# q k^T v in four 64x64 tiles of the TensorE array, k and v loaded and multiplied a batch at a time

## The chip, the cores and the metric

The kernel runs on one core of a Trainium2 chip. The metric is the device time of one execution in microseconds (us). Of three runs the kernel before took 1111.66 us in the median (1111.28 to 1112.53). The profile is of a further, profiled execution.

The engines have short names in the profile: PE is TensorE's matmuls, PEld its weight loads, DVE is VectorE, ACT is ScalarE, POOL is GpSimd, SP is SyncE, which issues nearly all DMAs here. A name with a q behind it (SPq) is an engine's queue.

## The reference

Two blocks, in float32. Attention without a softmax, for each of 8 batches and 8 heads (576 tokens of 64), with a root-mean-square norm; then a gated layer over all 4608 tokens:

```
kv  = einsum('bhsd,bhse->bhde', k, v)            # 64 x 64 a head
out = einsum('bhsd,bhde->bhse', q, kv)
x   = out / sqrt(mean(out*out, -1) + 1e-6) * g_norm     # (B,H,S,D) -> (4608, 512)
y   = (sigmoid(x @ w_gate) * (x @ w_val)) @ w_out       # d_ff = 1536
```

The weights arrive as 64-bit floats and are converted on the chip.

## The kernel before

**Attention goes by pairs of heads**, 32 in all, 4 a batch. `attention(n, at_ps)` (L211) returns the steps of pair n in their order, and each caller decides when a step runs:

- `kv_mm`: k^T v of both heads. The 576 tokens lie as 96 partitions with 6 tokens each, so a head takes six matmuls of 96 rows and 64 columns. Head 0 goes to PSUM partitions 0 to 63, head 1 to 64 to 127: two column tiles of the array (L221).
- `kv_out`: two copies on DVE put the two 64x64 results on the diagonal of a 128x128 tile that was cleared once (L227), and the loads of a later pair's k and v are issued (L79).
- `q_mm`, `q_out`: six transposes of q (L235), and a copy on ACT (L240), after which a later pair's q is loaded (L88).
- `u_mm`: q times k^T v of both heads at once, with the block-diagonal tile as the moving operand: five matmuls of 115 or 116 tokens (L250).
- `u_square`, `u_sum`, `u_root`, `u_norm`: the norm, on ACT, DVE, ACT, DVE (L254, L258, L262, L265 to L267).
- `x_mm`, `x_out`: five transposes back (L276), and copies on ACT into `xT`, the input of the gated layer (L285).

**The gated layer goes by chunks of 512 tokens**, nine of them. Chunk 0 is computed with plain matmuls (`Plain`, L380; `second`, L472) while the weights are still being converted. The order of the work in the first stage, with the attention of batches 0 and 1, is written out by hand as a list of tokens (`order`, L411): U3, for one, is `u_mm` of pair 3. `warm` tokens are matmuls without a use.

Chunks 1 to 8 run two layers of 7 instead of 8 products of half-size blocks. In `first_layer_fast` two blocks go side by side, one and two. Each has seven products of two matmuls, in the order p1, p6, p2, p7, p5, p4, p3. `product` (L529) issues the matmuls, and each product has an addition on DVE or a copy or sigmoid on ACT behind it. p1 and p2 accumulate into bank `pa`, p6, p7 and p4 into `pb`, p5 and p3 into `pc`. POOL makes the sums of weights (L515). `second_layer_fast` has products of six matmuls (L613) and stores its output tiles (`store`, L343).

**Attention of later batches fills slots.** Between the products there are calls of `slot()`, each of which takes one step from the queue `fill`. `feed(b)` puts the attention of batch b there, two pairs at a time; chunk c carries batch c+1, so chunks 1 to 6 carry batches 2 to 7, and 7 and 8 carry none. In chunk 1 the sums of the second layer's weights (L672, on DVE) are mixed in.

**PSUM has eight banks.** One tile of two banks (`at`, L353) serves all steps of attention, one after the other, so a step's result has to be read before the next step may write. Six single banks (`mm`, L370) serve the products.

**SBUF:** k and v of later pairs lie in two tiles each of the pool `sb`, q in one. Hidden activations come from the pool `hp`, 21 tiles of 128x512 under the tag gv, in turn; one chunk takes 21.

Of the kernel before, what the change touches and what calls it, by code (L numbers as in the profile page):

```python
# [2 lines left out]

# [16 lines left out]
def kernel(  # L20
# [21 lines left out]


    NU = 5
    M = S // NU
    MU = S - M * (NU - 1)
    UC = 192
    UX = M * 3
# [21 lines left out]
    def ahead(n, late):  # L70
        return (n + 4,) if n + 4 < NE else (n + late,) if n + late >= NE else ()

    def load_kv(n):
        if n >= B * NHP:
            return
        b, h0 = n // NHP, 2 * (n % NHP)
        for name, src in (("k", k), ("v", v)):
            t = (first if n < NE else sb).tile([NP, 2, NJ * HD], FP32, tag=name, name=name, bufs=4 if n < NE else 2)
            nc.sync.dma_start(out=t, in_=src[b, h0:h0 + 2].rearrange("h (p j) d -> p h (j d)", j=NJ))  # L79
            pairs[n][name] = t  # L80

    def load_q(n):
        if n >= B * NHP:
            return
        b, h0 = n // NHP, 2 * (n % NHP)
        t = (first if n < NE else sb).tile([NP, NJ, 2, HD], FP32, tag="q", name="q", bufs=4 if n < NE else 1)
        for e in range(2):
            nc.sync.dma_start(out=t[:, :, e, :], in_=q[b, h0 + e].rearrange("(p j) d -> p j d", j=NJ))  # L88
        pairs[n]["q"] = t

# [102 lines left out]
    kvs = [const.tile([P, P], FP32, name=f"kv{i}") for i in range(2)]  # L193
# [6 lines left out]
    for kv in kvs:  # L200
        nc.vector.memset(kv, 0.0)
# [9 lines left out]
    def attention(n, at_ps):  # L211

        b, m = divmod(n, NHP)
        d = {}

        def kv_mm():
            d["kv"] = ps = at_ps("kv")
            for j in range(NJ):
                js = slice(HD * j, HD * j + HD)
                for e in range(2):  # L220
                    nc.tensor.matmul(ps[HD * e:HD * e + HD, 0, 0:HD], pairs[n]["k"][:, e, js], pairs[n]["v"][:, e, js],  # L221
                                     start=(j == 0), stop=(j == NJ - 1))

        def kv_out():
            for e in range(2):
                es = slice(HD * e, HD * e + HD)
                nc.vector.tensor_copy(out=kvs[n % 2][es, es], in_=d["kv"][es, 0, 0:HD])  # L227
            for i in ahead(n, 2):
                load_kv(i)

        def q_mm():
            d["q"] = ps = at_ps("q")
            for j in range(NJ):
                c0 = NP * (j % JH)
                nc.tensor.transpose(ps[:, j // JH, c0:c0 + NP], pairs[n]["q"][:, j].rearrange("p e d -> p (e d)"),  # L235
                                    ident[0:NP, 0:NP])

        def q_out():
            d["qT"] = sb.tile([P, 2, JH * NP], FP32, tag="qT", name="qT")
            nc.scalar.copy(out=d["qT"], in_=d["q"][:, :, 0:JH * NP])  # L240
            for i in ahead(n, 1):
                load_q(i)

        def u_mm():

            ps = at_ps("u")
            d["u"] = ps[0:MU].rearrange("p i c -> p (i c)")[:, 0:NU * UC].rearrange("p (i c) -> p i c", c=UC)[:, :, 0:P]
            qT = d["qT"].rearrange("p i n -> p (i n)")
            for i in range(NU):
                nc.tensor.matmul(d["u"][:, i], qT[:, M * i:M * i + MU], kvs[n % 2], start=True, stop=True)  # L250

        def u_square():
            d["sq"] = sb.tile([MU, NU, P], FP32, tag="sq", name="sq")
            nc.scalar.activation(out=d["sq"], in_=d["u"], func=AF.Square)  # L254

        def u_sum():
            d["ms"] = sb.tile([MU, NU, 2], FP32, tag="ms", name="ms")
            nc.vector.tensor_reduce(out=d["ms"].rearrange("p i e -> p (i e)"),  # L258
                                    in_=d["sq"].rearrange("p i (e d) -> p (i e) d", d=HD), axis=AX.X, op=ALU.add)

        def u_root():
            nc.scalar.activation(out=d["ms"], in_=d["ms"], func=AF.Sqrt, bias=eps[0:MU], scale=1.0 / HD)  # L262

        def u_norm():
            nc.vector.reciprocal(d["ms"], d["ms"])  # L265
            d["xn"] = d["sq"]
            nc.vector.tensor_tensor(out=d["xn"].rearrange("p i (e d) -> p i e d", d=HD),  # L267
                                    in0=d["u"].rearrange("p i (e d) -> p i e d", d=HD),
                                    in1=d["ms"].unsqueeze(3).to_broadcast([MU, NU, 2, HD]), op=ALU.mult)

        def x_mm():
            d["x"] = ps = at_ps("x")
            for i in range(NU):
                m_ = MU if i == NU - 1 else M
                bank, c0 = divmod(M * i, UX)
                nc.tensor.transpose(ps[:, bank, c0:c0 + m_], d["xn"][0:m_, i, :], ident[0:m_, 0:m_])  # L276

        def x_out():

            s0 = 0  # L280
            while s0 < S:
                c, o = divmod(S * b + s0, G)
                i, r = divmod(s0, UX)
                n_ = min(G - o, (UX if i == 0 else S - UX) - r)
                nc.scalar.activation(out=chunk(c)[:, m, o:o + n_], in_=d["x"][:, i, r:r + n_], func=AF.Copy, scale=g_col)  # L285
                s0 += n_

        return [kv_mm, kv_out, q_mm, q_out, u_mm, u_square, u_sum, u_root, u_norm, x_mm, x_out]


# [6 lines left out]
    def feed(b, at_ps):  # L297

        for n in range(NHP * b, NHP * b + NHP, 2):
            both = []  # L300

            def tile_of(i, both=both):
                def ps(kind):
                    if kind != "kv":
                        return at_ps(kind)
                    if not both:
                        both.append(at_ps(kind))
                    return both[0][:, :, HD * i:HD * i + HD]
                return ps

            one, two_ = (attention(n + i, tile_of(i)) for i in range(2))

            def kv_of_both(one=one, two_=two_):
                one[0]()
                two_[0]()

            fill.extend([kv_of_both, one[1], two_[1]])
            for steps in (one, two_):

                fill.extend(steps[2:-2] + [lambda: None] * 2 + steps[-2:])  # L320
# [26 lines left out]

    psum_at = ctx.enter_context(tc.tile_pool(name="psum_at", bufs=1, space=bass.MemoryType.PSUM))
    psum_ctx = tc.tile_pool(name="psum0", bufs=1, space=bass.MemoryType.PSUM)
    psum0 = psum_ctx.__enter__()  # L350

    def at_ps(kind):
        return psum_at.tile([P, 2, 512], FP32, tag="at", name="at")  # L353
# [15 lines left out]
    def mm_ps():  # L369
        return psum.tile([P, 512], FP32, tag="mm", name="mm", bufs=6)  # L370
# [52 lines left out]
    two0 = at_ps(None)  # L423
    for token in order.split():
# [3 lines left out]
        if name == "b":  # L428
            if f not in blks:
# [4 lines left out]
                else:  # L434
                    t = at_ps(None) if f else two0
# [30 lines left out]
    for f in range(4, NFT):  # L466
        plain(0, f, (mm_ps(), mm_ps()))

    ps = [mm_ps() for _ in range(G // P)]
# [48 lines left out]
    def first_layer_fast(c):  # L518
        s, a = sx[c], quarters(c)

        def block(f):

            d = {}
            pa, pb, pc = (mm_ps()[:, h1] for _ in range(3))
# [8 lines left out]
            def p1():  # L533
                product(pa, bg[:, 0:NK], a[1, 1], True)
                d["sg"] = sg_tile()
                nc.scalar.copy(out=d["sg"][:, h2], in_=pa)  # L536

            def p6():
                product(pb, tw[f, 2], s[:, 1], True)
                d["h"] = gv_tile(c, f)  # L540
                tt(out=d["h"][:, h1], in0=pb, in1=d["sg"][:, h2], op=ALU.add)  # L541

            def p2():
                product(pa, bg[:, NK:], a[1, 2], False)
                nc.scalar.activation(out=d["sg"][:, h1], in_=pa, func=AF.Sigmoid)  # L545

            def p7():
                product(pb, tw[f, 3], a[2, 1], False)
                tt(out=d["h"][:, h2], in0=pb, in1=d["sg"][:, h2], op=ALU.add)  # L549

            def p5():
                product(pc, tw[f, 1], s[:, 0], True)
                tt(out=d["h"][:, h2], in0=pc, in1=d["h"][:, h2], op=ALU.add)

            def p4():
                product(pb, tw[f, 4], a[2, 2], False)
                tt(out=d["sg"][:, h2], in0=pb, in1=d["sg"][:, h2], op=ALU.add)  # L557
                nc.scalar.activation(out=d["sg"][:, h2], in_=d["sg"][:, h2], func=AF.Sigmoid)  # L558

            def p3():  # L560
                product(pc, bv[:, NK:], s[:, 2], False)
                tt(out=d["h"][:, h1], in0=pc, in1=d["h"][:, h1], op=ALU.add)  # L562
# [37 lines left out]
    def second_layer_fast(c):  # L600
        b = {(j, n): w2[:, NF2 * (j - 1):NF2 * j, DH * (n - 1):DH * n] for j in (1, 2) for n in (1, 2)}
        d1, d2 = slice(0, DH), slice(DH, DM)
        for g in range(2):
# [5 lines left out]
            pcs = [mm_ps()[:, 0:x.stop - x.start] for x in parts]  # L609
# [20 lines left out]
            for pc, x in zip(pcs, parts):  # L630
# [5 lines left out]
            store(c, 2 + g, o2)  # L636
            for pc, x in zip(pcs, parts):
# [42 lines left out]
    for c in range(1, NG):  # L680
        if c + 1 < B:
            feed(c + 1, at_ps)
        if c == 1:
# [3 lines left out]
            while w2_sums or steps:  # L687
                fill.append(w2_sums.popleft() if w2_sums and len(fill) % 7 in (3, 4) else steps.pop(0))
# [34 lines left out]
```

## Time and profile before

| what | value |
|---|---|
| median of three runs | 1111.66 us |
| the profiled execution: its time, its span | 1112.95 us, 1111.2 us |
| TensorE busy | 99% of the span |
| granted TensorE clock, mean | 0.998 |
| chunk 2 (with a batch's attention), first product to that of chunk 3 | 120.81 us |
| chunk 7 (without) | 108.78 us |
| mean duration of a record of L221, L250 | 224 ns, 273 ns |
| DMA, first two of 40 slices; mean over the span | 248 and 265 GB/s; 52 GB/s |

A line of the profile names the source line, the engine, the operation, the tiles as out<-in, the shape, and how many instructions of that kind it covers (x48). For matmuls, 96*64 means 96 rows and 64 columns of the array. Durations of matmuls are from entry to the end of the result, so neighbours overlap: how long one occupies the array is read from the difference of two starts. Each matmul of float32 shows up as two records, each transpose as one.

### The profile page before, as it was taken

The numbers are of one execution on the slowest core, as the hardware profiler recorded it, in microseconds if no ns is written. First come the engines' busy times: TensorE is split into PE (matmuls) and PEld (weight loads), VectorE is DVE, ScalarE is ACT, GpSimd is POOL, SyncE is SP. The second block draws the span as 40 slices with busy tenths as digits, with TensorE's granted clock in tenths as the row PEclk, the third lists the DMA queues.
The fourth block names the chain that finished last, engine by engine and source line by source line (L and its number), as shares of the span: only waits on it lengthen the run. The fifth ranks groups of instructions, "written<-read, shape, count | busy, mean of one in ns | idle before, by whom it ended". The sixth has DMA issues, their size and how long they took to land.

```text
span 1111.2 us, 15257 instructions
## 1 busy us (share of the span) xinstructions
PE 1101.6 (99%) x5830; PEld 920.2 (83%) x5830; DVE 571.6 (51%) x1159; ACT 318.7 (29%) x615; POOL 280.8 (25%) x390
## 2 busy tenths in 40 slices
PE   8999999999999999999999999999999999999998
PEld 7644458888888888888888888888888888888888
DVE  4887847753365415552455336551556256615541
ACT  4654323321243213330333124321333022101110
POOL 0000024540244204440343024420444044404420
PEclk9999999999999999999999999999999999999999
DMA  9954412021202020201211020203000000010001
GB/s 248 265 175 151 152 40 52 12 54 31 73 12 54 17 75 22 54 12 29 63 40 37 19 73 12 54 12 81 22 11 1 19 19 1 1 29 10 1 1 39
DMA packets 71912, 57.61 MB, mean 52 GB/s; under 512 B 40864, under 2 KB 65824, under 8 KB 71840
## 3 DMA queue, kind: packets, MB, share of 16 engines
q1 hardware_dynamic: 71584, 56.61, 19.2%
q8 instruction: 47, 0.77, 0.3%
q14 instruction: 25, 0.20, 0.1%
q10 hardware_dynamic: 256, 0.03, 0.0%
HBM read 47.19 MB, written 9.44 MB: 51 GB/s over the span
## 4 chain that ended last, share of the span: by engine, by line
PE 96%; DVE 1%; SPq 1%; DMA 1%; ACT 0%; issue 0%; DVEq 0%
PE mm L529 51%; PE mm L613 26%; PE mm L380 6%; PE mm L472 4%; PE at L250 2%; PE at L380 2%; PE at L221 2%; PE at L235 1%; PE at L276 1%; DMA q<-in_q_dram 1%; PE two L250 1%; PE two L221 0%; PE two L235 0%; PE two L276 0%; SPq L79 0%; SPq L88 0%
## 5 line engine op out<-in xcount | busy, mean ns | idle before, releaser
L515 POOL TENSOR_TENSOR tw<-gv 128x256 f32<-128x256 f32 x192 | 139.2, 737 | 780.2 <-PE mm L529 627.0
L529 PE MATMUL mm<-xT,tw 128*128 128x256 f32 x768 | 182.4, 381 | 0.9 <-DVE gv L541 0.9
L529 PE MATMUL mm<-sx,tw 128*128 128x256 f32 x768 | 182.6, 381 | 0.0
L529 PE MATMUL mm<-xT,gv 128*128 128x256 f32 x768 | 181.5, 380 | 0.0
L529 PEld LDWEIGHTS mm<-xT,gv 128*128 128x128 f32 x768 | 146.1, 191 | 19.7 <-issue 0.5
L529 PEld LDWEIGHTS mm<-sx,tw 128*128 128x128 f32 x768 | 144.4, 191 | 18.6
L529 PEld LDWEIGHTS mm<-xT,tw 128*128 128x128 f32 x768 | 143.8, 191 | 19.4 <-issue 1.2
L515 POOL TENSOR_TENSOR tw<-gv,tw 128x256 f32<-128x256 f32 x192 | 146.8, 785 | 0.0
L558 ACT ACTIVATE sg<-sg 128x256 f32<-128x256 f32 x96 | 39.7, 417 | 217.3 <-DVE sg L557 217.3
L549 DVE TENSOR_TENSOR gv<-mm,sg 128x256 f32<-128x256 f32 x96 | 40.8, 425 | 101.8 <-PE mm L529 101.8
L529 PE MATMUL mm<-sx,gv 128*128 128x256 f32 x384 | 90.9, 380 | 0.0
L613 PE MATMUL mm<-t2w,gv 128*128 128x256 f32 x384 | 89.0, 380 | 0.0
L613 PE MATMUL mm<-w,gv 128*128 128x256 f32 x384 | 88.3, 380 | 0.0
L613 PE MATMUL mm<-w,s 128*128 128x256 f32 (+1 forms) x408 | 88.3, 367 | 0.0
L613 PEld LDWEIGHTS mm<-w,s 128*128 128x128 f32 x408 | 74.2, 191 | 9.2
L613 PEld LDWEIGHTS mm<-t2w,gv 128*128 128x128 f32 x384 | 72.6, 191 | 9.4
L613 PEld LDWEIGHTS mm<-w,gv 128*128 128x128 f32 x384 | 72.6, 191 | 9.4
L529 PEld LDWEIGHTS mm<-sx,gv 128*128 128x128 f32 x384 | 72.2, 191 | 9.2
L536 ACT COPY sg<-mm 128x256 f32<-128x256 f32 x96 | 35.7, 372 | 151.4 <-PE mm L529 149.8
L565 DVE TENSOR_TENSOR gv<-gv,sg 128x512 f32<-128x512 f32 x96 | 78.6, 858 | 0.2
L562 DVE TENSOR_TENSOR gv<-mm,gv 128x256 f32<-128x256 f32 x96 | 40.8, 425 | 48.6 <-PE mm L529 48.2
L545 ACT ACTIVATE sg<-mm 128x256 f32<-128x256 f32 x96 | 36.2, 383 | 100.6 <-PE mm L529 100.6
(95 smaller groups left out, 1142.1 us busy)
## 6 DMA issues: line engine op xcount, KB each, us to landing
k<-in_k_dram SPq DMA_DIRECT2D x32, 288.0 KB, 4.6
v<-in_v_dram SPq DMA_DIRECT2D x32, 288.0 KB, 4.8
q<-in_q_dram SPq DMA_DIRECT2D x64, 144.0 KB, 3.0
st<-in_moe_w_gate_dram SPq DMA_DIRECT2D x12, 512.0 KB, 5.2
st<-in_moe_w_val_dram SPq DMA_DIRECT2D x12, 512.0 KB, 6.7
st<-in_moe_w_out_dram SPq DMA_DIRECT2D x12, 512.0 KB, 4.0
out_dram<-sg SPq DMA_DIRECT2D x23, 192.0 KB, 2.3
out_dram<-sg SPq DMA_DIRECT2D x24, 128.0 KB, 2.4
```

The lines of the kernel that those rows point to most:

```text
L250: nc.tensor.matmul(d["u"][:, i], qT[:, M * i:M * i + MU], kvs[n % 2], start=True, stop=True)
L380: nc.tensor.matmul(self.ps[i], w[("wg", "wv")[i], self.f][:, m, :], xT[self.c][:, m, :], start=(m == 0), stop=(m == NMT - 1), skip_group_c ...
L472: nc.tensor.matmul(ps[t], gv[0, f][:, P * t:P * t + P], w["wo", f], start=(f == 0), stop=(f == NFT - 1), skip_group_check=True)
L515: nc.gpsimd.tensor_tensor(out=tw[f, i], in0=b[in0], in1=b[in1] if isinstance(in1, tuple) else tw[f, in1], op=ALU.subtract)
L529: nc.tensor.matmul(ps, wt[:, m, :], xs[:, m, :], start=(new and m == 0), stop=(m == NK - 1), skip_group_check=True)
L536: nc.scalar.copy(out=d["sg"][:, h2], in_=pa)
L545: nc.scalar.activation(out=d["sg"][:, h1], in_=pa, func=AF.Sigmoid)
L549: tt(out=d["h"][:, h2], in0=pb, in1=d["sg"][:, h2], op=ALU.add)
L558: nc.scalar.activation(out=d["sg"][:, h2], in_=d["sg"][:, h2], func=AF.Sigmoid)
L562: tt(out=d["h"][:, h1], in0=pc, in1=d["h"][:, h1], op=ALU.add)
L565: tt(out=d["h"], in0=d["h"], in1=d["sg"], op=ALU.mult)
L613: nc.tensor.matmul(ps, hs(f), ws[:, f, :], start=(new and f == 0), stop=(f == NF2 - 1), skip_group_check=True)
```

## The change

- **k^T v**: the 64x64 results of a pair are kept one above the other (head 0 on partitions 0 to 63, head 1 on 64 to 127), in two tiles of two pairs each; no block-diagonal tile, one copy a pair or one for two pairs.
- **q k^T v** (`u_mm`): blocks of 64 tokens. Head e takes rows 64e to 64e+63 of the array, an even block writes PSUM partitions 0 to 63, an odd one 64 to 127: four tiles of 64x64, 20 matmuls a pair. Nine blocks of 64 make 576 tokens; a tenth repeats the last. The two heads write to different banks. In `feed` two pairs go in one step.
- **The norm and the transposes back** work on 128 partitions, five times 128 tokens for each head.
- **Loads from batch 2 on**: k and v of a batch come in nine tiles of `hp`: for each pair a tile of k and one of v, 512 tokens as 128 partitions with 4 tokens each, both heads; and one tile with the last 64 tokens of all heads. `load_late(b)` issues the twelve DMAs at once, in the second layer of chunk b-2 or, for batch 2, in chunk 0. The step `kv_mm` of a batch does all four pairs.
- **q** of later pairs has two tiles instead of one, and is loaded two pairs ahead.
- **PSUM**: attention takes two tiles of two banks in turn (`at`, `at1`), the products have four banks instead of six, and take a bank where they first write. The second layer of chunk 0 uses the four attention banks.
- **Slots**: 39 steps a batch (36 for batch 2) instead of 50, and the sums of chunk 1 stand further apart.

```diff
     def load_kv(n):
-        if n >= B * NHP:
+        if n >= NE:
             return
...
+    def load_late(b):
+        if b >= B:
+            return
+        mains = {}
+        for n in range(NHP):
+            for name, src in (("k", k), ("v", v)):
+                mains[n, name] = t = hp.tile([P, G], FP32, tag="gv", name="kv")
+                nc.sync.dma_start(out=t.rearrange("p (h c) -> p h c", h=2),
+                                  in_=src[b, 2 * n:2 * n + 2, 0:S4].rearrange("h (p j) d -> p h (j d)", j=NK4))
+        rest = hp.tile([P, G], FP32, tag="gv", name="kv")
+        for i, src in enumerate((k, v)):
+            for r in range(2):
+                nc.sync.dma_start(out=rest[PH * r:PH * r + PH, GH * i:GH * i + GH].rearrange("p (h d) -> p h d", d=HD),
+                                  in_=src[b, NHP * r:NHP * r + NHP, S4:S].rearrange("h p d -> p h d"))
+        kv_late[b] = mains, rest
...
         def kv_out():
-            for e in range(2):
-                es = slice(HD * e, HD * e + HD)
-                nc.vector.tensor_copy(out=kvs[n % 2][es, es], in_=d["kv"][es, 0, 0:HD])
-            for i in ahead(n, 2):
-                load_kv(i)
+            nc.vector.tensor_copy(out=kv, in_=d["kv"][:, 0, 0:HD])
+            load_kv(n + 4)
...
-            for i in range(NU):
-                nc.tensor.matmul(d["u"][:, i], qT[:, M * i:M * i + MU], kvs[n % 2], start=True, stop=True)
+            for i in range(2 * NU):
+                t0 = min(PH * i, S - PH)
+                r = PH * (i % 2)
+                for e in range(2):
+                    es = slice(HD * e, HD * e + HD)
+                    nc.tensor.matmul(d["u"][r:r + PH, e, HD * (i // 2):HD * (i // 2) + HD], qT[es, t0:t0 + PH], kv[es],
+                                     start=True, stop=True)
...
-                nc.tensor.transpose(ps[:, bank, c0:c0 + m_], d["xn"][0:m_, i, :], ident[0:m_, 0:m_])
+                bank, c0 = divmod(P * i, UX)
+                nc.tensor.transpose(ps[:, bank, c0:c0 + P], d["xn"][:, P * i:P * i + P], ident)
...
+        def kv_mm():
+            mains, rest = kv_late[b]
+            tiles = [at_ps("kv") for _ in range(2)]
+            d["kv"] = tiles
+            for n in range(NHP):
+                for j in range(NK4):
+                    for e in range(2):
+                        c = slice(NK4 * HD * e + HD * j, NK4 * HD * e + HD * j + HD)
+                        nc.tensor.matmul(tiles[n // 2][HD * e:HD * e + HD, n % 2, 0:HD], mains[n, "k"][:, c],
+                                         mains[n, "v"][:, c], start=(j == 0), stop=False)
+            for i in range(NHP // 2):
+                for r in range(2):
+                    for e in range(2):
+                        n, rs, c = NHP // 2 * r + i, slice(PH * r, PH * r + PH), HD * (2 * i + e)
+                        nc.tensor.matmul(tiles[n // 2][HD * e:HD * e + HD, n % 2, 0:HD], rest[rs, c:c + HD],
+                                         rest[rs, GH + c:GH + c + HD], start=False, stop=True)
...
+            def u_of_both(one=one, two_=two_):
+                one[U]()
+                two_[U]()
+
+            fill.extend([one[Q], one[Q_OUT], two_[Q], two_[Q_OUT]])
+            if n == NHP * b:
+                fill.extend([idle] * (0 if early else 3) + [kv_mm, kv_out])
+            fill.extend([u_of_both, one[U_SQUARE], two_[U_SQUARE], one[U_SUM], two_[U_SUM], one[U_ROOT], one[U_NORM],
+                         two_[U_ROOT], two_[U_NORM], one[X], one[X_OUT], two_[X], two_[X_OUT]])
...
     def at_ps(kind):
-        return psum_at.tile([P, 2, 512], FP32, tag="at", name="at")
+        if next(turns) % 2 == 0:
+            return at0_ps()
+        return psum.tile([P, 2, 512], FP32, tag="at1", name="at1")
...
-        return psum.tile([P, 512], FP32, tag="mm", name="mm", bufs=6)
+        return psum.tile([P, 512], FP32, tag="mm", name="mm", bufs=4)
...
+        if f == NFT - 2:
+            load_late(2)
...
             store(c, 2 + g, o2)
+            if g == 1:
+                load_late(c + 2)
...
-                fill.append(w2_sums.popleft() if w2_sums and len(fill) % 7 in (3, 4) else steps.pop(0))
+                fill.append(w2_sums.popleft() if w2_sums and len(fill) % 7 in ((3, 4) if len(fill) > 28 else (3,)) else steps.pop(0))
```

## The prediction

> **What bounds the kernel now.** I read the engine table first, then the busy time by stage, then the timeline of TensorE around one pass of attention, last its list of waits.
>
> ```profile
> PE 1101.6 (99%) x5830; PEld 920.2 (83%) x5830; DVE 571.6 (51%) x1159; ACT 318.7 (29%) x615; POOL 280.8 (25%) x390
> ```
>
> TensorE is busy all the time, the next engine half of it. The stages show what attention costs there (columns: length, then busy time and instructions of PE, PEld, DVE, ACT, POOL, then clock, DMA share and GB/s):
>
> ```profile
> 162.53:286.37 123.84, 121.83 (x686) 106.75 (x685) 67.63 (x137) 32.40 (x70) 39.75 (x48) 1.00 0.16 40
> 407.19:528.00 120.81, 120.81 (x685) 106.82 (x685) 56.90 (x130) 36.23 (x72) 33.39 (x48) 1.00 0.15 39
> 890.44:999.22 108.78, 108.78 (x505) 96.04 (x505) 52.33 (x110) 16.84 (x41) 36.05 (x48) 1.00 0.04 10
> ```
>
> A chunk with attention in its slots takes 120.81 us, one without 108.78. So the attention of a batch costs 12.03 us, and all of it on TensorE, which has no gap. Chunk 1 takes 123.84, 3.0 us more. The timeline of TensorE in chunk 2 splits the 12.03:
>
> ```profile
> 407.02 1.89 PE L529 MATMUL mm<-xT,gv 128*128 128x256 f32 x8
> 408.84 1.62 PE L221 MATMUL at<-v,k 96*64 96x64 f32 x48
> 410.39 2.00 PE L529 MATMUL mm<-sx,tw 128*128 128x256 f32 x8
> 412.22 1.89 PE L529 MATMUL mm<-xT,gv 128*128 128x256 f32 x8
> 413.95 1.89 PE L529 MATMUL mm<-xT,tw 128*128 128x256 f32 x8
> 415.68 0.66 PE L235 MATMUL at<-ident,q 96*128 96x96 f32 x6
> 416.17 1.92 PE L529 MATMUL mm<-sx,tw 128*128 128x256 f32 x8
> 417.93 1.89 PE L529 MATMUL mm<-xT,tw 128*128 128x256 f32 x8
> 419.66 1.26 PE L250 MATMUL at<-kv,qT 128*116 128x128 f32 x10
> 420.75 1.89 PE L529 MATMUL mm<-sx,gv 128*128 128x256 f32 x8
> ```
>
> I read differences of starts, since the durations overlap. An undisturbed group of 8 takes 1.73 us (412.22 to 413.95). A matmul leaves two records (the 24 of two pairs' k^T v are x48), two passes over the array; a transpose leaves one.
> - q k^T v (L250): 420.75 - 419.66 = 1.09 us a pair, 109 ns a record of 128 columns, no loss beside it.
> - k^T v of two pairs (L221): 1.55 us, and its neighbours take 1.82 and 1.83 instead of 1.73: 1.74 us in all.
> - q transposes 0.49 + 0.03; the transposes of x (L276, same view elsewhere) 0.50 + 0.03.
>
> 4 x (1.09 + 0.52 + 0.53) + 2 x 1.74 = 12.04: the split closes. Inside the k^T v run, ever longer looks from 408.80 on (to 408.86, 409.00 and 409.02) hold
>
> ```profile
> 408.84 0.28 PE L221 MATMUL at<-v,k 96*64 96x64 f32 x2
> 408.84 0.34 PE L221 MATMUL at<-v,k 96*64 96x64 f32 x4
> 408.84 0.39 PE L221 MATMUL at<-v,k 96*64 96x64 f32 x6
> ```
>
> Records come two at a time, 7 ns apart, and each such pair takes 58.4 ns: 29.2 ns a record, 48 x 29.2 = 1.40 us. So entering and leaving the half-width tiles costs 1.74 - 1.40 = **0.34 us a run**. That 7 ns decides the forecast. In the full array no record starts before its predecessor's columns are through (216 or 109 ns). Both passes of one matmul need the same 64 columns of the array, so two records 7 ns apart must belong to different tiles: each tile works through its own matmuls, and the other tile's don't queue behind them. The rows don't name tile or pass; this is inferred.
>
> **The change, part by part.** Its own time is 1112.95 us for a span of 1111.2; the runs' median is 1111.66. I take differences and put them on the median.
>
> *q k^T v in four tiles.* Before 10 records of 109 ns; now 20 matmuls of 64 columns, 40 records. With four tiles at the measured 58.4 ns a record each: 40 x 14.6 = 0.58 us a pair. Two pairs a run: 1.17 + 0.34 = 1.51 against 2.18, so -0.67; 12 runs: **-8.1**. In the first stage pairs go alone: 0.58 + 0.34 = 0.92 against 1.09, -0.17 each; pairs 0 and 1 are followed by waits on loads (q 1.3 us, v 0.6), so six count: **-1.0** (0 to -1.4).
>
> Here two rules of the Trainium skill speak against the change, both on the page "TensorE: Matmul & The Clock Gate". Part 3 says that matmuls start and end strictly in program order. Then the second pass of a tile holds up every tile behind it, never more than two tiles overlap, and 80 records cost 80 x 29.2 + 0.34 = 2.68 us: +0.5 a run, and the sum below becomes +5.4. Part 2 of the same page ("Back-to-back issue gap") puts an issue floor of about 25 ns under small matmuls; over all tiles that is 80 x 25 + 0.34 = 2.34 a run, and the sum about -1. The row has starts 7 ns apart, below that floor and not explained by that order; I take the row. No row shows four tiles, nor tiles on different rows of the array; their pace lies between 14.6 and 29.2, and I take the lower end by the row it is nearest to: a record in L221's two tiles takes 58.4 ns where half of L250's 109 would be 54.6, so two tiles slow each other by 7% at most.
>
> *k^T v of a batch in one run.* Before 2 x 1.74 = 3.48. Now 32 matmuls of 128 rows in two column tiles: 64 x 29.2 = 1.87. Then 8 of 64 rows in four tiles: 16 x 14.6 = 0.23 (0.47 at two). One entry and exit, 0.34; a further switch between the two shapes, not in the trace, 0 to 0.34: I take 0.15. Sum 2.59, -0.89 a batch, six batches: **-5.3**.
>
> *x transposed in 128s.* Five of 128 columns for five of 115: 0.50 x 128/115 = 0.555, +0.055 a pair; 24 pairs and the six early ones: **+1.65**. The other engines see the same 640 elements a partition.
>
> *Four banks for attention, four for the products.* Two of chunk 1's three waits go with a single attention tile, the transposes of q standing behind a copy out of it:
>
> ```profile
> PE mm L529 <- DVE gv L541: 0.9, 1, 0.9
> PE at L235 <- DVE kv L227: 0.8, 1, 0.8
> PE at L235 <- ACT xT L285: 0.3, 1, 0.3
> ```
>
> By starts, chunk 1 loses 0.49, 1.01 and 0.98 us to them. With two tiles in turn and the weight sums of the second layer spread wider I take **-1.5** (0 to -2.5). Against it, products now get a bank back after four tiles, not six: p5 waits for p2's sigmoid, the next block's p1 for p4's addition, its p6 for p3's. Each is four products back, with three products, 3 x 0.864 = 2.6 us, between the end of the one and the start of the other. That is the distance that p6 to p7 and p1 to p2 have today, on DVE and on ACT, without a wait in chunks 2 to 8. The worst case is a square root on ACT just before p2's sigmoids: two table loads of 1.28, 0.30 and two sigmoids of 0.38 are 3.6 us against 3.5 available. I take **+0.8** for all new waits (0 to 3). Behind a late p5 the whole of TensorE stands.
>
> *Loads.* Twelve DMAs a batch (eight of 256 KB, four of 64 KB) replace eight of 288 KB. They now stand on SP ahead of the last store of a chunk, at 0.34 to 0.46 us of SP each (k and v in the timeline): 5 us. Its buffer is needed again some 15 us into the next chunk, so nothing waits. The 2.36 MB take 9.3 us at the 255 GB/s of the first slices (start 2.6 us before the chunk's end, the last of them freed 1.7 before it); k^T v is eight slots in, 12.1 + 1.7 + 1.0 = 14.8 us. Some 6 us of cover, so nothing; without it a batch would pay the excess. In the first stage k and v of pairs 8 and 9 no longer load, q of 9 does. Batch 2 now loads beside the weights at f = 10, with 14 us of slack there (three staged units at 6.9 us, less 4 to 7 a unit). The q of a pair is loaded two pairs ahead on SP instead of one: earlier, nothing waits. Fewer copies of k^T v (218 ns each) and no clearing of it: DVE, not on the path.
>
> Sum: -8.1 - 1.0 - 5.3 + 1.65 - 1.5 + 0.8 = -13.45; 1111.66 - 13.45 = **1098.2 us**.
>
> **Rivals.**
> 1. *Two tiles at a time* (the program order above): u +5.9 (12 x 0.49), early +2.5, k^T v -3.9, the rest +0.95: +5.4, **1117**. For it: the page, and that no row shows four. Against it: the 7 ns. It decides from a pace of 25.8 ns a record on, where 1200 x pace (80 x 12 + 40 x 6) - 26.6 equals the 4.4 gained elsewhere.
> 2. *Partly overlapping tiles*, 20 ns a record: 80 x 20 + 0.34 = 1.94 a run, -2.9; early about 0: -7, **1105**.
> 3. *Waits for banks.* 24 square roots at 0.3 us more each eat 7 us: **1105**; the change turns slower from 0.56 us each. For it: the 3.6 against 3.5 above; against it: most roots fall in slots where the sigmoids go first.
> 4. *Loads too late*: at half the rate 18.6 us against 17.4 of cover, about 1 us in five batches: **1103**. The DMA queues are nearly empty there.
>
> **How the numbers follow.** The forecast case 70% (own range 1095 to 1102), rival 1 11%, rival 2 10%, rivals 3 and 4 9%. From 1094.5 (all bounds on the good side) to 1107 holds the first and most of 2 to 4. A measurement of this kernel tells 0.2%, 2.2 us, from no change. Faster 0.84: the first, rival 2 and half of 3 and 4; within 0.2% 0.03; slower 0.13.
>
> **What would show it.** A run of x80 for q k^T v about 1.2 us long with 0.3 lost beside it, records four to 58 ns; k^T v x80 about 2.3 long; chunks of 118.8 us instead of 120.8, chunk 1 near 120.5; those without attention still 108.8; no wait of TensorE for ACT at p5. A run of 2.4 to 2.7 us would prove rival 1; waits of PE on ACT or DVE in chunks 2 to 7, rival 3; on DMA, rival 4.

## The result and the profile after

The changed kernel takes 1097.71 us in the median of four runs (1097.39 to 1098.79), the kernel before 1111.97 in the runs beside it. The ratio is 0.9874 with a 95% interval of 0.9857 to 0.9891. The forecast was 1098.2, with a range of 1094.5 to 1107. The profiled execution of the changed kernel took 1098.79 us for a span of 1096.9; the span before was 1111.2, so 14.3 us have gone in these two.

The engine table of the changed kernel:

```profile
PE 1088.6 (99%) x6694; PEld 901.9 (82%) x6694; DVE 567.1 (52%) x1113; ACT 312.8 (29%) x609; POOL 283.3 (26%) x390
```

TensorE is still busy all the time, now with 864 more records in less time. The busy time by stage shows where the time came from. First the kernel after: chunks 1, 2, 3 and, from 876.16 on, chunk 7, which carries no attention (columns as in the prediction):

```profile
161.94:282.37 120.43, 119.20 (x789) 104.04 (x788) 65.22 (x131) 30.19 (x65) 37.82 (x48) 1.00 0.09 21
282.37:401.10 118.73, 118.73 (x790) 104.21 (x789) 56.98 (x124) 35.83 (x72) 34.27 (x48) 1.00 0.15 40
401.10:519.83 118.73, 118.73 (x790) 104.21 (x789) 56.98 (x124) 35.84 (x72) 34.27 (x48) 1.00 0.15 40
...
876.16:984.94 108.78, 108.78 (x506) 95.76 (x505) 52.32 (x110) 15.55 (x40) 36.05 (x48) 1.00 0.04 10
```

The same view of the kernel before, cut at the first product of a chunk, which for chunk 1 is 0.16 us closer than the stretch shown in the prediction:

```profile
162.53:286.21 123.68, 121.67 (x685) 106.59 (x684) 67.63 (x137) 32.40 (x70) 39.75 (x48) 1.00 0.16 39
286.21:407.02 120.81, 120.81 (x685) 106.83 (x684) 56.88 (x130) 36.23 (x72) 33.39 (x48) 1.00 0.15 39
```

Five chunks (2 to 6) save 2.08 us each, 10.4 in all. Within a trace these five agree to 0.01 us, and chunk 7 takes 108.78 in the trace of every run of this document, so differences of a chunk between two traces are hardly blurred by chance. Chunk 1 saves 3.25. Its first product starts 0.59 us earlier (161.94 against 162.53). Chunks 7 and 8, without attention, are what they were. 10.4 + 3.25 + 0.59 = 14.2: the split closes.

The timeline of TensorE around the same work in the changed kernel, in chunk 3 (L578 are products of the gated layer, L332 and L338 are k^T v, L271 is q k^T v):

```profile
412.51 1.89 PE L578 MATMUL mm<-sx,gv 128*128 128x256 f32 x8
414.23 1.89 PE L578 MATMUL mm<-xT,gv 128*128 128x256 f32 x8
416.05 2.08 PE L332 MATMUL at<-kv 128*64 128x64 f32 x64
418.07 0.46 PE L338 MATMUL at<-kv 64*64 64x64 f32 x16
418.46 1.99 PE L578 MATMUL mm<-sx,tw 128*128 128x256 f32 x8
420.29 1.89 PE L578 MATMUL mm<-xT,gv 128*128 128x256 f32 x8
422.11 1.40 PE L271 MATMUL at<-kv,qT 64*64 64x64 f32 x80
423.44 1.99 PE L578 MATMUL mm<-xT,tw 128*128 128x256 f32 x8
425.27 1.89 PE L578 MATMUL mm<-sx,tw 128*128 128x256 f32 x8
```

By differences of starts, q k^T v of two pairs runs 1.33 us (422.11 to 423.44), and the groups beside it take 1.82 and 1.83 us instead of 1.73: 1.52 in all, where the forecast had 1.51. k^T v of a batch runs 2.41 (416.05 to 418.46) and costs its neighbours 0.19: 2.60, forecast 2.59.

Windows of growing length into that L271 run, from 422.10 to 422.14, 422.26 and 422.32, hold

```profile
422.11 0.29 PE L271 MATMUL at<-kv,qT 64*64 64x64 f32 x4
422.11 0.34 PE L271 MATMUL at<-kv,qT 64*64 64x64 f32 x8
422.11 0.40 PE L271 MATMUL at<-kv,qT 64*64 64x64 f32 x12
```

Four records start within 0.04 us, then four more, then four more. In steady state such a group of four takes 58 ns, 14.6 ns a record: four tiles work side by side, each at the pace that it had when there were two.

All waits of TensorE for another engine in the changed kernel are these:

```profile
PE two L240 <- DMA v<-in_v_dram: 1.8, 1, 1.8
PE at L506 <- POOL ident masks.py:199: 1.4, 1, 1.4
PE mm L578 <- DVE gv L592: 1.2, 2, 0.8
PE two L271 <- ACT qT L256: 0.6, 2, 0.3
PE two L251 <- DMA q<-in_q_dram: 0.3, 1, 0.3
```

Only one row lies behind the first stage: twice in chunk 1, p7 waits for the addition of p6 on DVE. The two rows of chunk 1 in which q's transposes waited for a copy are gone. None of the waits that four product banks could have brought has appeared, nor, behind the first stage, one for the loads of k and v.

### The profile page after: what moved, and what is told of

Its sections match the earlier page's. It is cut to its first block, busy times and chain, and to the rows that moved or that the text cites. A ratio compares the mean times of both kernels' runs of the same rounds, so it can differ in the third digit from the quotient of the medians.

```text
span 1096.9 us, 17004 instructions
## 1 busy us (share of the span) xinstructions
PE 1088.6 (99%) x6694; PEld 901.9 (82%) x6694; DVE 567.1 (52%) x1113; ACT 312.8 (29%) x609; POOL 283.3 (26%) x390
## 4 chain that ended last, share of the span: by engine, by line
PE 97%; DMA 1%; DVE 1%; SPq 0%; issue 0%; ACT 0%; DVEq 0%
PE mm L578 52%; PE mm L664 26%; PE mm L427 6%; PE at L522 4%; PE at L427 2%; PE at L271 1%; PE at L298 1%; PE at L332 1%; PE at L251 1%; DMA q<-in_q_dram 1%; PE two L271 0%; PE two L240 0%; PE two L298 0%; PE two L251 0%; DMA g_col<-in_g_norm_dram 0%
## 5 line engine op out<-in xcount | busy, mean ns | idle before, releaser
L578 PE MATMUL mm<-xT,tw 128*128 128x256 f32 x768 | 182.3, 380 | 1.2 <-DVE gv L592 1.2
L578 PE MATMUL mm<-sx,tw 128*128 128x256 f32 x768 | 182.4, 380 | 0.0
L578 PE MATMUL mm<-xT,gv 128*128 128x256 f32 x768 | 181.7, 379 | 0.0
L578 PEld LDWEIGHTS mm<-xT,tw 128*128 128x128 f32 x768 | 143.9, 190 | 20.9 <-issue 2.0
L578 PEld LDWEIGHTS mm<-xT,gv 128*128 128x128 f32 x768 | 144.9, 190 | 19.7 <-issue 0.5
L578 PEld LDWEIGHTS mm<-sx,tw 128*128 128x128 f32 x768 | 144.2, 190 | 19.1
L565 POOL TENSOR_TENSOR tw<-gv,tw 128x256 f32<-128x256 f32 x192 | 149.0, 797 | 0.0
L578 PE MATMUL mm<-sx,gv 128*128 128x256 f32 x384 | 91.3, 381 | 0.0
L617 DVE TENSOR_TENSOR gv<-gv,sg 128x512 f32<-128x512 f32 x96 | 85.3, 927 | 0.0
L578 PEld LDWEIGHTS mm<-sx,gv 128*128 128x128 f32 x384 | 72.4, 190 | 10.0
```

Source lines behind the costliest of these rows:

```text
L565: nc.gpsimd.tensor_tensor(out=tw[f, i], in0=b[in0], in1=b[in1] if isinstance(in1, tuple) else tw[f, in1], op=ALU.subtract)
L578: nc.tensor.matmul(ps, wt[:, m, :], xs[:, m, :], start=(new and m == 0), stop=(m == NK - 1), skip_group_check=True)
L617: tt(out=d["h"], in0=d["h"], in1=d["sg"], op=ALU.mult)
```

## Experiments

The theory: the gain is TensorE's own time, because tiles of the array run side by side; a switch into small tiles and back costs a fixed 0.34 us; the banks give only what chunk 1 had lost. The rivals: only two tiles overlap and the gain has another source; the banks make the gain, or cost waits; the loads are late. Chunk times below are from the busy time by stage of each run's own trace, cut at the first product of a chunk.

**q k^T v put back.** The changed kernel with q k^T v alone in the full array:

```diff
-            for i in range(2 * NU):
-                t0 = min(PH * i, S - PH)
-                r = PH * (i % 2)
-                for e in range(2):
-                    es = slice(HD * e, HD * e + HD)
-                    nc.tensor.matmul(d["u"][r:r + PH, e, HD * (i // 2):HD * (i // 2) + HD], qT[es, t0:t0 + PH], kv[es],
-                                     start=True, stop=True)
+            for i in range(NU):
+                t0 = min(P * i, S - P)
+                nc.tensor.matmul(d["u"][:, i], qT[:, t0:t0 + P], kv, start=True, stop=True)
```

with k^T v copied to the diagonal of four cleared 128x128 tiles, and the views of the norm to match.

> The changed kernel with q k^T v alone put back into the full array (block-diagonal k^T v, five matmuls of 128 tokens and 128 columns a pair), still two pairs a run. Theory: a run is 20 records of 109 ns = 2.18 us without loss beside it, against 1.52 now: +0.66 x 12 = +8, and 0 to 1 in the first stage: 1105.5 to 1107. Rival (strict order, only two tiles overlap; the gain comes from elsewhere): no slower than the changed kernel.

Measured: 1106.75 us (1106.71 to 1106.92), ratio to the kernel before 0.9952 (0.9939 to 0.9966). Chunks 2 and 3:

```profile
283.30:403.45 120.15, 120.15 (x669) 106.28 (x668) 58.28 (x130) 36.07 (x72) 34.27 (x48) 1.00 0.15 39
403.45:523.60 120.15, 120.15 (x670) 106.28 (x669) 58.29 (x130) 36.08 (x72) 34.27 (x48) 1.00 0.14 40
```

1.42 us a chunk more than the changed kernel, 0.71 a run of two pairs, and 1.42 x 6 = 8.5 of the 14.3. That is the share of q k^T v in the gain. In chunk 3 its run of 20 records takes 2.23 us from start to start (424.37 to 426.60), only 0.05 more than 20 x 109 ns, and the group behind it an undisturbed 1.73: no switch of 0.34 shows here, and the small tiles win in spite of theirs. No run puts k^T v back by itself; its share of the gain, 0.88 a batch, is read from starts.

**Two tiles of 64 rows and 128 columns.** Another way to use both halves of the rows:

```diff
-            for i in range(2 * NU):
-                t0 = min(PH * i, S - PH)
-                r = PH * (i % 2)
-                for e in range(2):
-                    es = slice(HD * e, HD * e + HD)
-                    nc.tensor.matmul(d["u"][r:r + PH, e, HD * (i // 2):HD * (i // 2) + HD], qT[es, t0:t0 + PH], kv[es],
-                                     start=True, stop=True)
+            for i in range(NU):
+                t0 = min(P * i, S - P)
+                for e in range(2):
+                    es = slice(HD * e, HD * e + HD)
+                    nc.tensor.matmul(d["u"][:, e, HD * i:HD * i + HD], qT[es, t0:t0 + P], kv[es], start=True, stop=True)
```

The fifth transpose back is placed to match.

> The changed kernel with q k^T v in two tiles of 64 rows and 128 columns instead of four of 64 by 64: ten matmuls a pair, 64 columns streamed, weights of 128 columns. If a tile's pace is set by the columns that stream through it (58.4 ns for 64), 40 records in two tiles cost 40 x 29.2 = 1.17 us a run, as now: 1098. If it is set by loading 128 columns of weights (107 ns between the first two matmul starts behind a k^T v run, where nothing hides the load), 40 x 54 = 2.2 and 0.34: +1.0 x 12 and +0.5 x 6: 1110 to 1114. I expect the second.

Measured: 1112.79 us, ratio 1.0013 (1.0003 to 1.0022), so no better than before the change. Chunks 2 and 3 take 120.83 us. The run of 40 records, from the timeline:

```profile
427.75 2.45 PE L270 MATMUL at<-kv,qT 64*128 64x64 f32 x40
430.13 1.99 PE L576 MATMUL mm<-xT,tw 128*128 128x256 f32 x8
```

2.38 us instead of 1.33. Records still come in pairs 7 ns apart, so tiles on different rows do overlap; but a pair takes 112 ns (from one start to the next of the same parity), although only 64 columns stream through, which took 58 in tiles 64 columns wide. The weights are twice as wide, and the trace of their loads (PEld) speaks for the second expectation. Windows here from 427.74 to 427.85 and 427.87, then in the changed kernel from 422.10 to 422.16 and 422.19, hold

```profile
427.75 0.19 PEld L270 LDWEIGHTS at<-kv,qT 64*128 64x128 f32 x2 [0.33 <-issue]
427.75 0.30 PEld L270 LDWEIGHTS at<-kv,qT 64*128 64x128 f32 x4 [0.33 <-issue]
422.11 0.15 PEld L271 LDWEIGHTS at<-kv,qT 64*64 64x64 f32 x4 [0.33 <-issue]
422.11 0.21 PEld L271 LDWEIGHTS at<-kv,qT 64*64 64x64 f32 x8 [0.33 <-issue]
```

Each tile's second load starts 108 ns behind its first with 128 columns of weights, and 55 ns behind it with 64: about the distances at which the matmuls of a tile then follow each other (112 and 58). That nothing else of the wider tile slows them was not tested apart. The 107 ns in the expectation are such a distance too, of the first two loads behind a k^T v run (410.39 and 410.50 in the kernel before); the first two matmuls there start 0.32 us apart, not 107 ns.

**The same matmuls in another order.** All of one tile, then all of the next:

```diff
-            for i in range(2 * NU):
-                t0 = min(PH * i, S - PH)
-                r = PH * (i % 2)
-                for e in range(2):
-                    es = slice(HD * e, HD * e + HD)
+            for e, i in [(e, i) for r in range(2) for e in range(2) for i in range(r, 2 * NU, 2)]:
+                t0 = min(PH * i, S - PH)
+                r = PH * (i % 2)
+                for es in [slice(HD * e, HD * e + HD)]:
```

> The changed kernel with the same matmuls of q k^T v in another order: all five of one tile, then all five of the next. Theory (each tile works through its own matmuls as far as TensorE looks ahead in its program): if it looks ahead without limit, a run stays 1.33 us and the time 1098. If it looks no further than the next tile, ten records follow each other on one tile at 58.4 ns: 80 x 58.4 = 4.7 us and 0.34, +3.5 x 12 and +1.75 x 6 to 8, so 1098 + 52 to 56 = 1150. From what was issued ahead in k^T v of the kernel before I expect some 16 records of look-ahead: between, 1110 to 1130. Rival (a run costs its columns wherever they go): 1098.

Measured: 1129.98 us in one run, 32 above the changed kernel, between the two ends and near the upper end of what I had expected. A run takes 3.55 us instead of 1.33:

```profile
435.57 3.62 PE L270 MATMUL at<-kv,qT 64*64 64x64 f32 x80
439.12 1.99 PE L577 MATMUL mm<-xT,tw 128*128 128x256 f32 x8
```

2.22 x 12 = 26.6, and chunk 1 begins 4.5 us later: together 31.1 of the 31.3 between the spans. Windows into this run from 435.56 on, to 435.60, 435.70, 435.95 and 435.99:

```profile
435.57 0.27 PE L270 MATMUL at<-kv,qT 64*64 64x64 f32 x1
435.57 0.33 PE L270 MATMUL at<-kv,qT 64*64 64x64 f32 x2
435.57 0.56 PE L270 MATMUL at<-kv,qT 64*64 64x64 f32 x6
435.57 0.67 PE L270 MATMUL at<-kv,qT 64*64 64x64 f32 x8
```

Records start one at a time, the second 107 ns behind the first and the next 58 ns apart, until the seventh; the eighth start comes 5 ns behind it. That record lasts 267 ns, as the first of the run does, where the others last 218. There are eight such long records in the run, for two pairs of four tiles, and they start 404 ns apart. So each is the first of a tile's ten, and it starts beside the seventh of the tile before, past three that still wait. TensorE does start matmuls out of program order when their tile is free, but it looks only a few records ahead, not 16. The time follows: 107 + 5 x 58 + 5 ns make such a step of about 404; seven steps, the last tile's ten records and 0.15 us to the next product make the 3.55. In the changed kernel's order, tile by tile in turn, the fourth tile's first record also has to pass just three waiting ones (the second passes of the first three tiles, if a matmul's two passes stand side by side in the program, which the rows don't name). An order with two matmuls a tile, which would test the count, was not tried.

**One pair a run.**

```diff
-            fill.extend([u_of_both, one[U_SQUARE], two_[U_SQUARE], one[U_SUM], two_[U_SUM], one[U_ROOT], one[U_NORM],
+            fill.extend([one[U], two_[U], one[U_SQUARE], two_[U_SQUARE], one[U_SUM], two_[U_SUM], one[U_ROOT], one[U_NORM],
```

> The changed kernel with q k^T v of one pair a slot instead of two: the same matmuls, 12 more entries to and exits from the four tiles. Theory (0.34 us a run, whatever is in it): +0.34 x 12 = +4.1 us, 1101.8, chunks of 119.4 us. Rival (entering costs nothing of its own, the run's length is records alone): no change.

Measured: 1103.89 us, ratio 0.9924 (0.9905 to 0.9943): +6.2, more than the 4.1. Chunks 2 and 3 take 119.91 us, +1.18. The timeline of chunk 3 splits it:

```profile
421.07 1.89 PE L578 MATMUL mm<-xT,gv 128*128 128x256 f32 x8
422.89 0.81 PE L271 MATMUL at<-kv,qT 64*64 64x64 f32 x40
423.63 2.00 PE L578 MATMUL mm<-xT,tw 128*128 128x256 f32 x8
425.56 0.81 PE L271 MATMUL at<-kv,qT 64*64 64x64 f32 x40
426.30 1.99 PE L578 MATMUL mm<-sx,tw 128*128 128x256 f32 x8
428.13 1.89 PE L578 MATMUL mm<-xT,tw 128*128 128x256 f32 x8
...
435.04 1.89 PE L578 MATMUL mm<-xT,gv 128*128 128x256 f32 x8
437.16 1.97 PE L578 MATMUL mm<-xT,tw 128*128 128x256 f32 x8 [0.24 <-DVE gv L592]
438.96 1.89 PE L578 MATMUL mm<-sx,tw 128*128 128x256 f32 x8
```

From 421.07 to 428.13 there are 7.06 us; three groups of 1.73 and 80 records at 14.6 ns make 6.36. Two switches cost 0.70, so 0.35 each: the fixed price holds, and one more run costs one more of it. Twice a chunk that is 0.70. The other 0.48 is a new wait, once in each of chunks 2 to 6: the group at 435.04 takes 2.12 and the next 1.80. The step more in the queue has moved the second pair's sum on DVE (0.81 us) between the sums of the hidden activations and p6's addition, for which p7 waits. I had not counted that a slot more moves everything behind it.

**k^T v in two runs.** Pairs 0 and 2 in one step, 1 and 3 in the next:

```diff
-        def kv_mm():
+        def kv_mm(half):
...
-            for n in range(NHP):
+            for n in (half, NHP // 2 + half):
...
-            for i in range(NHP // 2):
+            for i in (half,):
...
-                fill.extend([idle] * (0 if early else 3) + [kv_mm, kv_out])
+                fill.extend([idle] * (0 if early else 2) + [lambda: kv_mm(0), lambda: kv_mm(1), kv_out])
```

> The changed kernel with k^T v of a batch in two steps of two pairs each, one slot apart (one idle slot less ahead of them). Theory: one more entry and exit a batch, 0.34, and one more switch from 128x64 to 64x64 tiles, 0.15: +0.49 x 6 = +2.9 us, 1100.6. Rival (the gain of k^T v is in its fewer records alone): no change.

Measured: 1100.36 us (1098.85 to 1100.74), ratio 0.9888 (0.9873 to 0.9903). Chunks 1 and 2:

```profile
160.38:279.99 119.61, 119.47 (x789) 104.25 (x788) 64.31 (x131) 35.62 (x69) 37.38 (x48) 1.00 0.09 21
279.99:399.22 119.23, 119.23 (x789) 104.34 (x788) 56.99 (x124) 35.84 (x72) 34.28 (x48) 1.00 0.15 40
```

+0.50 us in chunk 2, forecast 0.49. By the chunks the whole is 5 x 0.50 - 0.82 = 1.7; the medians are 2.65 apart, and the profiled execution is the fastest of its four. Chunk 1 is 0.82 shorter than in the changed kernel: it has one slot more ahead of the later steps, and no product waits for DVE in it. That this is the shift, and not the shorter pieces, was not tested.

**The banks alone.** The kernel before with the attention tiles in turn and four product banks:

```diff
     def at_ps(kind):
-        return psum_at.tile([P, 2, 512], FP32, tag="at", name="at")
+        if next(turns) % 2 == 0:
+            return at0_ps()
+        return psum.tile([P, 2, 512], FP32, tag="at1", name="at1")
...
-        return psum.tile([P, 512], FP32, tag="mm", name="mm", bufs=6)
+        return psum.tile([P, 512], FP32, tag="mm", name="mm", bufs=4)
```

and `pa`, `pb`, `pc` taken where they first write.

> The kernel before with one part of the change alone: attention takes two PSUM tiles of two banks in turn, the products have four banks instead of six and take them where they first write. Theory (the gain comes from TensorE's own time in q k^T v and k^T v): only chunk 1 changes; its waits of the q transposes behind copies out of the one attention tile (0.98 and 0.49 us by starts) go, so -1.5 us (-0.5 to -2.5), and chunks 2 to 7 stay at 120.8. Rival (the banks make the gain): -5 us or more, spread over the chunks. Rival (four product banks cost waits): slower, waits of TensorE for ACT or DVE at p5, p1 or p6 in chunks 2 to 6.

Measured: 1110.00 us (11 runs), ratio 0.9986 (0.9977 to 0.9994).

```profile
161.41:283.50 122.09, 121.23 (x685) 106.50 (x684) 67.64 (x137) 32.44 (x70) 39.77 (x48) 1.00 0.16 40
283.50:404.32 120.82, 120.82 (x686) 106.56 (x685) 56.89 (x130) 36.27 (x72) 33.39 (x48) 1.00 0.15 39
```

Chunk 1 goes from 123.68 to 122.09, -1.59, and chunk 2 stays. In chunk 1 TensorE waits once for the addition at p6, no more for the copies out of the attention tile. Fewer product banks cost nothing, and the banks are worth about a tenth of the gain.

**The old spacing of the weight sums in chunk 1.**

```diff
-                fill.append(w2_sums.popleft() if w2_sums and len(fill) % 7 in ((3, 4) if len(fill) > 28 else (3,)) else steps.pop(0))
+                fill.append(w2_sums.popleft() if w2_sums and len(fill) % 7 in (3, 4) else steps.pop(0))
```

> The changed kernel with the second layer's weight sums of chunk 1 put as close together as before (two in seven slots from the start). Chunk 1 went from 123.84 to 120.43 us, 2.1 of it as every chunk. Theory (the other 1.3 come from the second attention tile): chunk 1 stays within 0.5 us. Rival (they come from the wider spacing): chunk 1 grows by 1.3.

Measured: 1097.70 us, chunk 1 120.29 (120.43 in the changed kernel). The spacing is worth nothing here. The run above gives the second attention tile as the source of chunk 1's extra gain; but by the run with k^T v in two parts, one slot more or less moves chunk 1 as much, so the split of that 1.17 us is not shown.

**k^T v three slots earlier.**

```diff
-                fill.extend([idle] * (0 if early else 3) + [kv_mm, kv_out])
+                fill.extend([kv_mm, kv_out])
```

> The changed kernel without the three idle slots ahead of k^T v of a batch, so that it runs 5.2 us earlier. In the changed kernel's chunk 3 the last loads are issued 6.0 us into the chunk and k^T v starts 14.8 us into it; here it would start 9.6 us in. With about 3 us from issue to landing for the last loads (9 us in) nothing waits: no change (0 to +1 us a chunk where they are late, five chunks). If the loads land as late as 9.3 us of transfer after their last issue, TensorE waits for a DMA at k^T v, up to 5 us a chunk, +25.

Measured: 1097.04 us in two runs, chunks 2 and 3 at 118.76 and 118.74 instead of 118.73. k^T v now starts 9.8 us into chunk 3 (409.17, with the chunk's first product at 399.39), and nothing waits for its loads. Their cover in the changed kernel is at least the 5 us that these slots took.

## Why the prediction was right

- **q k^T v, -8.1.** Right in mechanism and size: 1.52 us a run against 1.51, and putting it back costs 8.5. The reading of the 7 ns, that records starting together belong to different tiles and that a tile's second pass doesn't hold up the tiles behind it, is borne out by four starts in 0.04 us and by the order by tile, where starts pass waiting records.

  The two rules of the Trainium skill that the prediction set against itself (page "TensorE: Matmul & The Clock Gate") do not hold across tiles here: by the strict program order of Part 3 a run would have cost 2.68 us, by the issue floor of about 25 ns in Part 2 ("Back-to-back issue gap"), taken over all tiles, 2.34; the row has 14.6 ns a record, and the measurement decides.

  One step of the argument was weaker than it looks. In strict order, with the two passes of a matmul side by side, records would come in pairs every 58 ns too, the second pass of one matmul beside the first of the next, at the same 29.2 ns a record; only the run's very first record would stand alone. So of the rows before, the first window alone, with two records at once, spoke against that order. The order by tile shows the passing whichever way the passes lie. And the "about -1" under the floor left the last 16 records of k^T v at 14.6 ns; at 25 they add 1.0, and the sum is about 0.
- **k^T v, -5.3.** 2.60 a batch against 2.59. The unknown switch between the two shapes, taken at 0.15 between 0 and 0.34, shows in the timeline: L332's 64 records take 2.02 us (416.05 to 418.07) where 64 x 29.2 ns make 1.87. Cutting the run in two costs 0.50, which is 0.35 and 0.15 again.
- **The transposes of x, +1.65.** Over-sized. Per chunk the q k^T v and k^T v terms make 2 x 0.66 + 0.88 = 2.20, and 2.08 was saved, so some 0.12 is left for four transposes, 0.03 a pair instead of 0.055. The timeline has 0.04: they take 0.55 instead of 0.50, and the group behind them 1.73 instead of 1.74. So the loss beside them was 0.01 in chunks 2 to 6 before, not the 0.03 of the prediction. Over six chunks the term was 0.4 to 0.6 us too large.
- **Chunk 1, -1.5, and new waits, +0.8.** The banks alone give -1.59, in the changed kernel 3.25 - 2.08 = 1.17. The new waits are zero: the list of waits has no product in chunks 2 to 8. The near miss that I had worked out at p5, 3.6 us against 3.5, shows no wait. The spreading of the weight sums, which I had named as a part of the -1.5, does nothing.
- **First stage, -0.67** (-1.0 and the transposes' 0.33). The first product of chunk 1 came 0.59 us earlier. That can't be told from chance: with the same first stage it started at 161.94, 161.02, 160.38, 160.19 and 161.58 in five executions (the changed kernel, one pair a run, k^T v in two runs, k^T v earlier, old spacing). The waits for the loads of q and v vary there.
- **Loads at no cost.** Right, by the run with k^T v three slots earlier. The last store of a chunk behind the twelve DMAs made nobody wait.

Between the medians 14.26 us have gone, 0.8 more than the 13.45 of the sum: waits that did not come (0.8) and the transposes (about 0.5) were priced too high, and chunk 1's gain, 0.3 too high as well, hides a part of that. The time itself came out 0.5 off because the sum started from 1111.66 and not from 1111.97: that closeness is in part luck.

The rivals were not met: two tiles at a time by the starts, partial overlap by the 14.6 ns, banks and loads by the list of waits.

## What to carry to other kernels

Small matmuls in tiles of the array pay a fixed price to get in and out (0.35 us here), so group them into one run, and give neighbouring matmuls different tiles: the same 80 records took 1.33 us in turn and 3.55 tile by tile. Narrow tiles did better than wide ones for a short moving operand, 1.33 us against 2.38, so look at the width of the weights, whose loads went at that pace, and not only at the columns that stream. Where TensorE is the bound and fully dense, a change to it is worth its difference of starts, and one slot more or less can bring or remove a wait elsewhere.

## What the runs showed of the hardware

- Matmuls of different tiles start out of program order, but the look-ahead is short: with ten records a tile in a row, the next tile's first started only beside the seventh, and a step from tile to tile took 404 ns.
- In 64x64 tiles four records start 7 ns apart and the group takes 58 ns, the same as two records took in two tiles: the third and fourth tile cost nothing in pace.
- In two tiles of 64x128 a pair of records of 64 columns takes 112 ns, about twice as long as in tiles 64 columns wide. The first two weight loads of a tile start 108 ns apart there, 55 ns in the narrow tiles.
